# One table of names sets the order of every operation in a fused attention and mixture-of-experts kernel; the change replaces that table

## The chip, the cores and the metric

The kernel runs on one core of one Trainium2 chip. The metric is the time of one execution in microseconds of device time, as the median of several runs; lower is better. Engines are named as the profile names them: PE (matmul), PEld (weight loads for it), DVE (vector), ACT (activation), POOL and SP (the last issues transfers here and computes nothing).

## The reference, cut to what matters

Two parts run one after the other. The first is causal attention over 4 batches, 8 heads, 768 positions and 64 features; four heads in a fixed pattern (`is_retrieval` is 1 for heads 0, 2 and 6) see all earlier positions or, if not flagged, the first 4 and the last 64 only. The second treats the attention's output as 3072 tokens of 512 features and sends them through a soft mixture of 8 experts with 4 slots each.

```
scores = scale * q @ k.T ; a = softmax(where(mask, scores, -1e9)) ; x = a @ v        # per batch and head
logits = x @ phi                                                                      # 3072 x 32
slot_input = softmax(logits, over tokens).T @ x                                       # 32 x 512
slot_out[e] = relu(slot_input[e] @ w1[e]) @ w2[e]                                     # 8 experts
out = softmax(logits, over slots) @ slot_out                                          # 3072 x 512, float32
```

In: q, k and v of 6.3 MB each, w1 and w2 of 16.8 MB each, all float32. Out: 6.3 MB.

## The kernel before, in words

**Stages.** Batches b are 0 to 3. In a batch, heads are worked in pairs (n and n+4), so there are 16 pairs, p = 4b + n. For each pair the scores are made in five groups of two matmuls or more, exponentiated, masked, multiplied with v and normalised. After four pairs of a batch, the logits of the batch are made and its share of the slot inputs is added up. After the last batch come the experts and then the output, in 24 row blocks.

**Transfers in.** Every load of q, k, v and the weights is one instruction on POOL's queue and converts float32 to bfloat16 on the way. There are 12 buffers of 8 KB per partition (`slots`); w2 of experts 4 to 7 goes into memory that attention has left (`qk`, `vx`, `xv`). The last weight, w2 of expert 7, comes in two halves of 256 columns, `Lw15h0` and `Lw15h1`. Stores go out from SP's queue.

**Order.** A class `Plan` collects operations with names, dependences and buffers. Each engine runs its own operations strictly in the order in which their names stand in one string, `ORDER`; a suffix gives the engine where there is a choice (`/A` is ACT, `/D` is DVE, `/P` is POOL):

```
for word in ORDER.split():
    name, _, e = word.partition("/")
    o = by.pop(name)
    o.eng = {"A": "ACT", "D": "DVE", "P": "POOL"}[e] if e else o.engs[0]
```

The order decides also which of several equal buffers an operation gets, since `run` hands them out in that order. Dependences are met by semaphores and do not change.

**Names.** These are used below.

- `Lq0`, `Lk1.32`, `Lw3`: loads (line 244). Lw0 to Lw7 are w1, Lw8 to Lw15 are w2. Raw rows of q, k and v of batches 1 to 3 are packed into shared buffers, so `Lk1.32` and `Lv1.0` fill one buffer together.
- `Tq1.3`, `Eq1.3`: transposes of raw rows on PE (L421) and the copy of their result to `qk` or `xv` (L237 on ACT, L239 on DVE).
- `QK.p.g`, `EX.p.g`, `MK.p.g`: scores of a group (PE, L451), exponential (ACT, L518), mask (DVE, L463). `QX.b`, `EXX.b` are the same for one leftover block per pair (L534).
- `V2.p`, `VB.p`, `VF.p`: v turned to rows (PE, L482), its copy to `vx`, and a masked copy `vf` (L498) for the blocks far from the diagonal. `VF` may run on POOL or DVE.
- `PV.p.i`, `NM.p`: product with v for row block i (PE, L566), normalisation (DVE, L577 and L579).
- `XT`, `XE`, `LG`, `EL`, `TE`, `EG`, `DS`, `SA`: transposes of the attention output, logits, their exponential, and the slot sums (PE L591, L605, L627, L662; ACT L618; DVE L671 and L673).
- `SI`, `H.e.c`, `HR`, `TH`, `HE`: slot inputs, first expert matmul (PE, L734), relu (ACT L744 or DVE L746), transposes (L755) and their copy.
- `W2.e`: second expert matmul (PE, L793); `W2.7.0` and `W2.7.1` need `Lw15h0` and `Lw15h1`. `SO.0`, `SO.1`: its two column halves scaled (ACT, L808, or the same on DVE).
- `EE.b`, `RWa`, `RWRa`: the token weights put in output order, their sums (L778) and reciprocals (L782).
- `OMf0L`, `OEf0L`, `STl0.0`: output matmul of row block 0, left half (PE, L818), its scaling (ACT L824 or DVE L826), and the store (SP, L862). Row blocks 0 to 7 are done in halves L and R; 8 to 23 whole. L needs only `SO.0`. There are 11 stores: four of 256 KB, four of 512 KB, three of 1 MB.
- `Z..`: matmuls on zeros that only keep PE active (L359).

Of the kernel before, what the change touches and what calls it, by code (L numbers as in the profile page):

```python
# [25 lines left out]
QK.1.1 PV.0.3 PV.0.4 QK.1.3 Lk1.32 VF.1/D MK.1.2 EX.1.1 PV.0.5 Lv1.0 QK.2.3 VB.2/D Lv1.64 Tq1.0 NM.0 MK.1.1
EX.1.3 QK.2.4 Tq1.1 PV.1.0 EX.2.3 MK.1.3 PV.1.1 Ek1.0.0/D EX.2.4 QK.1.4 PV.1.2 PV.1.3 QK.2.1 Eq1.0/D Ek1.1.0/D
Eq1.1/D Tq1.2 EX.1.4 QK.2.0 MK.1.4 Tk1.2 Eq1.2/D EX.2.1 Lw1 Ek1.2.0/D PV.1.4 Lw2 VF.2/P Ek1.2.32/D MK.2.3
EX.2.0 Ev1.2.0/A PV.1.5 NM.1 MK.2.0 QK.2.2 Z67 EX.2.2 Tk1.1 Lq2 Ev1.1.0/D Lk2 QK.3.0 Ek1.1.32/D Tk1.0 PV.2.0
VF.3/P QK.3.1 EX.3.0 Ev1.0.0/D Tk1.3 QK.3.2 EX.3.1 Ek1.0.32/D MK.2.2 MK.2.1 Tq1.3 MK.2.4 QK.3.3 Lv2.0 PV.2.1  # L30
PV.2.2 PV.2.3 MK.3.0 EX.3.2 MK.3.1 Lv2.32 QK.3.4 Lq3.0 PV.2.4 PV.2.5 Ev1.3.0/D Ek1.3.0/D EX.3.3 Eq1.3/D EX.3.4
Z65 MK.3.2 NM.2 QK.4.2 QK.4.1 V2.5 PV.3.0 Ek1.3.32/A PV.3.1 MK.3.3 MK.3.4 EX.4.2 V2.4 PV.3.2 QK.4.3 PV.3.3
VB.4/D PV.3.4 PV.3.5 EX.4.1 Lq3.64 QK.4.0 MK.4.2 VB.5/D EX.4.3 XT.2 EX.4.0 NM.3 XT.0 VF.4/P Z66 XE.0/D QK.5.0
MK.4.0 MK.4.1 XE.2/A QK.5.2 EX.5.0 PV.4.0 XT.3 XT.1 PV.4.1 EX.5.2 PV.4.2 XE.3/D QK.4.4 XE.1/D MK.4.3 Tv1.0
Eq2.0/D LG.0 EX.4.4 Tv1.1 Ev1.0.64/D Tv1.3 MK.5.2 EL.0 Ev1.1.64/A MK.5.0 Eq2.1/D QK.5.1 PV.4.3 TE.0 Eq2.3/D
Lw3 QX.1 Ev1.3.64/D EX.5.1 MK.4.4 EXX.1 Tv1.2 EG.0/D DS.0 QK.5.3 VF.5/P MK.5.1 PV.4.4 PV.4.5 Eq2.2/D
Ev1.2.64/A QK.6.2 SA.0 V2.6 EX.5.3 QK.5.4 NM.4 V2.7 VB.6/D PV.5.0 EX.6.2 EX.5.4 Lw4 PV.5.1 QK.6.1 Tk2.0 MK.6.2
EX.6.1 PV.5.2 Lw5 VB.7/D MK.5.3 QK.6.0 Ev2.0.0/D Tk2.1 PV.5.3 QK.6.3 MK.5.4 Ek2.0/D MK.6.1 Lk3 EX.6.0 PV.5.4
EX.6.3 Ek2.1/D Ev2.1.0/D VF.6/P PV.5.5 QK.7.1 Tk2.3 MK.6.0 EX.7.1 QK.6.4 Tk2.2 NM.5 QK.7.0 MK.6.3 Ek2.3/D
Ev2.3.0/D EX.6.4 MK.6.4 PV.6.0 MK.7.1 PV.6.1 Ev2.2.0/D PV.6.2 PV.6.3 QK.7.2 XT.5 PV.6.4 PV.6.5 EX.7.0 XE.5/D  # L40
QK.7.4 MK.7.0 VF.7/P EX.7.2 XT.4 Ek2.2/A NM.6 EX.7.4 XE.4/D QK.7.3 EX.7.3 V2.8 PV.7.0 PV.7.1 MK.7.2 QK.8.0
Tv2.0 PV.7.2 MK.7.4 QK.8.1 VB.8/D Ev2.0.32/D Eq3.0.0/D Tv2.2 EX.8.0 QK.8.2 XT.6 MK.7.3 Ev2.2.32/D EX.8.1
PV.7.3 MK.8.0 XE.6/D Eq3.2.0/D QK.8.3 EX.8.2 EX.8.3 PV.7.4 Lv3 PV.7.5 MK.8.1 NM.7 Tv2.1 QK.9.0 Tv2.3 Eq3.1.0/A
Lw6 VF.8/P QX.2 EX.9.0 Ev2.1.32/D Lw7 Ev2.3.32/D PV.8.0 XT.7 Eq3.3.0/D Lw8 EXX.2 PV.8.1 XE.7/D MK.8.2 QK.8.4
V2.9 VB.9/D V2.11 PV.8.2 EX.8.4 VB.11/A LG.1 MK.8.4 VF.9/P MK.8.3 QK.9.1 PV.8.3 EL.1 V2.10 PV.8.4 VF.11/D
MK.9.0 VB.10/D EX.9.1 QK.9.3 TE.1 PV.8.5 EG.1/D EX.9.3 MK.9.1 QK.9.2 DS.1 QK.9.4 NM.8 Tq3.0 SA.1 EX.9.2 PV.9.0
EX.9.4 PV.9.1 Eq3.0.64/D QK.10.1 XT.8 QK.10.2 Ek3.0/D MK.9.2 XE.8/D Tq3.1 PV.9.2 EX.10.1 MK.9.3 QK.10.0 MK.9.4
Lw9 Ek3.1/D Tq3.2 EX.10.2 PV.9.3 Eq3.2.64/D Ek3.2/D QK.10.3 VF.10/P PV.9.4 PV.9.5 Eq3.1.64/D EX.10.0 MK.10.2
QK.11.0 Tq3.3 EX.10.3 QK.10.4 NM.9 MK.10.0 EX.11.0 Tv3.0 QK.11.2 PV.10.0 MK.10.1 Ev3.0/D PV.10.1 MK.10.3
PV.10.2 EX.10.4 QK.11.1 MK.11.0 MK.10.4 EX.11.2 XT.9 PV.10.3 EX.11.1 Eq3.3.64/D QK.11.4 Lw10 Ek3.3/D PV.10.4  # L50
EX.11.4 XE.9/D PV.10.5 QK.12.1 Tv3.3 EX.12.1 NM.10 QK.11.3 Tv3.2 QK.12.0 EX.11.3 Ev3.3/D PV.11.0 MK.11.1 Tv3.1
EX.12.0 QX.3 Ev3.2/D MK.11.2 XT.10 Ev3.1/D PV.11.1 QK.12.2 EXX.3 MK.11.3 MK.12.0 V2.12 EX.12.2 MK.11.4 VB.12/D
PV.11.2 QK.12.4 MK.12.1 PV.11.3 PV.11.4 EX.12.4 Lw11 XE.10/D QK.12.3 VF.12/P EX.12.3 PV.11.5 QK.13.1 Lw12
NM.11 MK.12.3 V2.13 MK.12.2 QK.13.0 MK.12.4 XT.11 XE.11/D EX.13.1 PV.12.0 PV.12.1 EX.13.0 QK.13.2 PV.12.2
PV.12.3 QK.13.4 EX.13.2 MK.13.0 EX.13.4 PV.12.4 PV.12.5 QK.13.3 LG.2 MK.13.2 NM.12 VB.13/A VF.13/D MK.13.1
EX.13.3 V2.14 QK.14.1 VB.14/D PV.13.0 V2.15 EL.2 EX.14.1 PV.13.1 MK.13.3 QK.14.0 PV.13.2 QK.14.2 VB.15/D
MK.13.4 MK.14.1 Lw13 PV.13.3 EX.14.0 EX.14.2 PV.13.4 VF.14/P VF.15/P QK.14.3 PV.13.5 MK.14.0 QK.14.4 EX.14.3
TE.2 NM.13 EX.14.4 XT.12 EG.2/D QK.15.0 PV.14.0 MK.14.3 PV.14.1 MK.14.2 MK.14.4 XT.13 XE.13/D QK.15.1 PV.14.2
EX.15.0 EX.15.1 PV.14.3 QK.15.2 XE.12/D PV.14.4 PV.14.5 EX.15.2 QK.15.3 EX.15.3 MK.15.1 QK.15.4 MK.15.0 NM.14
MK.15.2 DS.2 PV.15.0 EX.15.4 MK.15.3 PV.15.1 MK.15.4 XT.14 PV.15.2 PV.15.3 Lw14 XE.14/A SA.2 PV.15.4 PV.15.5  # L60
LTa LGa.3 NM.15 XT.15 XE.15/D Z1 LTb ET LGb.3 Z2 EL.3 DS.3 SA.3 RC Z3 SI Z4 SIE EE.3/D H.0.1 H.0.0 EE.0/D
H.1.0 HR.0.1/D HR.0.0/A TH.0 H.1.1 EE.1/D HE.0/D W2.0 W2.1 HR.1.0/A HR.1.1/A Lw15h0 TH.1 HE.1/D W2.2 W2.3 W2.4
EE.2/D W2.5 W2.6 Lw15h1 W2.7.0 SO.0/A RWa RWRa OMf0L OMf1L OEf1L/D RWb OMf2L RWRb OMf3L OMf4L OEf2L/D OEf0L/A
OEf3L/A OMf5L W2.7.1 OEf4L/A OMf6L SO.1/A OMf7L STl0.0 OMf0R OMf1R OMf2R OEf6L/A OEf5L/D OEf1R/A STl0.2 OMf3R
OEf7L/D OEf0R/D OMf4R OMf5R OMf6R STl1.0 OMf7R OMf8 OEf3R/A OMf9 OEf6R/A OEf2R/D OEf4R/D OMf10 OMf11 STl1.2
# [835 lines left out]
```

## Time and profile before

| | |
|---|---|
| median of 3 runs | 149.55 us (149.5 to 149.68) |
| the profiled execution | 149.39 us, of which the span of the trace is 147.6 us |
| PE, DVE, ACT, POOL busy | 128.8, 115.9, 104.9, 36.4 us |
| granted PE clock, mean | 0.964 |
| moved by the transfer queues | 32.89 MB in bytes written, 223 GB/s over the span |

The profiled execution is 1.79 us longer than its span, and 0.16 us shorter than the median. Loads are counted by the bytes that they write (bfloat16), which is half of what they read. Busy time of PE is modelled from pipelined matmuls, so it is no measure of how near PE is to its peak.

### The profile page before, as it was taken

The page shows a single profiled execution, that of the slowest core. Times are in us where ns is not written, and L with a number is a line of the kernel's source. Part 1 is how long each engine was busy: PE and PEld are TensorE (multiplying, and loading weights), DVE is VectorE, ACT ScalarE, POOL GpSimd, SP SyncE. Part 2 cuts the span into 40 slices and gives each one's busy share as a digit, 9 for nine tenths or more (in the row PEclk, how much of TensorE's full clock was granted, in tenths as well). Part 3 has the DMA queues.
Part 4 walks back from the last instruction along what each step waited for, and adds up shares of the span by engine and source line. Part 5 has one row for each costly group of instructions (what it writes and reads, how often), then busy time and mean ns, then how long its engine had stood idle before and what let it go on. Part 6 is the DMA issues. An engine that isn't in the chain of part 4 may idle for free.

```text
span 147.6 us, 5037 instructions
## 1 busy us (share of the span) xinstructions
PE 128.8 (87%) x2196; PEld 82.2 (56%) x2204; DVE 115.9 (78%) x273; ACT 104.9 (71%) x129; POOL 36.4 (25%) x59
## 2 busy tenths in 40 slices
...
DMA  3999999999999999999999999999999999889995
GB/s 31 197 217 220 216 208 213 212 222 215 212 212 214 214 216 223 220 215 209 206 218 220 213 215 215 218 218 218 215 215 218 218 206 190 119 276 361 422 413 233
DMA packets 10373, 32.89 MB, mean 223 GB/s; under 512 B 1392, under 2 KB 5488, under 8 KB 8048
## 3 DMA queue, kind: packets, MB, share of 16 engines
...
q14 instruction: 4, 0.03, 0.1%
...
## 4 chain that ended last, share of the span: by engine, by line
PE 34%; DMA 24%; DVE 18%; ACT 8%; POOL 4%; issue 4%; ACTq 0%; POOLq 0%; DVEq 0%
DMA slot<-in_v_dram 12%; DMA qk<-in_moe_w_dram 12%; PE ps L566 9%; PE ps L451 8%; PE ps L421 7%; DVE pt L463 6%; ACT pt L518 4%; DVE xv L579 4%; ACT slot L824 3%; PE ps L818 2%; POOL slot L244 2%; PE ps L591 2%; PE ps L605 2%; DVE vx L239 1%; DVE qk L239 1%
## 5 line engine op out<-in xcount | busy, mean ns | idle before, releaser
L518 ACT ACTIVATE pt<-ps 128x1024 bf16<-128x1024 f32 x80 | 77.4, 1035 | 8.0 <-PE ps L451 7.2
L463 DVE TENSOR_TENSOR pt<-pt,msk 128x512 bf16<-128x512 bf16 (+1 forms) x80 | 38.2, 505 | 0.7 <-ACT pt L518 0.7
L451 PE MATMUL ps<-qk 64*128 64x512 bf16 (+3 forms) x256 | 32.5, 309 | 0.2
L566 PEld LDWEIGHTS <-pt 128*128 128x128 bf16 x640 | 25.1, 97 | 9.4 <-issue 6.2
L566 PE MATMUL ps<-vx,pt 128*128 128x65 bf16 x352 | 28.5, 193 | 1.0 <-DVE pt L463 0.4
L421 PE MATMUL ps<-ident,slot 128*64 128x128 bf16 (+1 forms) x640 | 22.8, 216 | 2.6 <-DMA slot<-in_q_dram 1.1
L498 POOL TENSOR_TENSOR vf<-vx,fm 128x528 bf16<-128x528 bf16 x12 | 13.9, 1164 | 44.5 <-DVE vx L239 42.1
L421 PEld LDWEIGHTS <-slot 128*64 128x64 bf16 (+1 forms) x640 | 17.7, 109 | 10.7 <-issue 8.7
L566 PE MATMUL ps<-vf,pt 128*128 128x65 bf16 x288 | 22.8, 195 | 0.0
L239 DVE COPY qk<-ps 128x768 bf16<-128x768 bf16 (+2 forms) x35 | 15.3, 466 | 6.0 <-PE ps L421 4.8
L359 PE MATMUL ps<-zero 128*128 128x512 bf16 x51 | 15.2, 412 | 1.8 <-DVE zero L350 1.2
L579 DVE TENSOR_TENSOR xv<-ps,rs 128x768 bf16<-128x768 f32 x16 | 15.3, 957 | 0.6
L451 PEld LDWEIGHTS <-qk 64*128 64x128 bf16 x256 | 9.3, 94 | 8.2 <-issue 2.7
L239 DVE COPY xT<-ps 128x768 bf16<-128x768 bf16 (+1 forms) x16 | 8.9, 569 | 3.2 <-PE ps L755 2.3
L244 POOL DMA_DIRECT2D slot<-in_moe_w_dram x12 | 7.1, 589 | 14.5 <-PE ps L421 12.0
L824 ACT ACTIVATE slot<-ps,rrow 128x512 f32<-128x512 f32 (+1 forms) x17 | 8.8, 588 | 2.2 <-PE ps L818 2.2
L826 DVE TENSOR_SCALAR slot<-ps,rrow 128x256 f32<-128x256 f32 (+1 forms) x15 | 8.5, 603 | 1.8 <-PE ps L818 1.1
L818 PE MATMUL ps<-msk,xv 128*128 128x256 bf16 (+1 forms) x31 | 8.0, 381 | 1.7 <-ACT slot L824 0.9
L239 DVE COPY xv<-ps 128x768 bf16<-128x768 bf16 (+2 forms) x21 | 8.9, 430 | 0.7 <-PE ps L421 0.4
L359 PEld LDWEIGHTS <-zero 128*128 128x128 bf16 x58 | 5.3, 103 | 7.5 <-issue 2.7
L237 ACT COPY qk<-ps 128x768 bf16<-128x768 bf16 (+1 forms) x5 | 3.5, 713 | 7.0 <-PE ps L421 7.0
L239 DVE COPY vx<-ps 128x768 bf16<-128x768 bf16 x14 | 7.7, 553 | 0.6 <-PE ps L482 0.6
...
## 6 DMA issues: line engine op xcount, KB each, us to landing
slot<-in_moe_w_dram POOLq DMA_DIRECT2D x12, 1024.0 KB, 22.7
out_dram<-slot SPq DMA_DIRECT2D x3, 1024.0 KB, 6.2
...
qk<-in_moe_w_dram POOLq DMA_DIRECT2D x1, 1024.0 KB, 19.1
```

The costliest lines, as they stand in the source:

```text
L239: nc.vector.tensor_copy(dst, src)
L244: emit=lambda o: e.dma_start(dst(), src))
L359: nc.tensor.matmul(scb[buf.slot][:, 0, :], zero[:, 0:128], zero, start=True, stop=True)
L421: nc.tensor.transpose(t[64 * i:64 * (i + 1), :, s, :], rv[:, i, 8 * c + s, :], ident[0:rows, 0:rows])
L451: nc.tensor.matmul(scb[sc.slot][:, i, c:c + 128 * nb], kk, qq.rearrange("p b c -> p (b c)"), start=True, stop=True)
L463: e.tensor_tensor(pT[:, :, 0:w], pT[:, :, 0:w], mh[:, :, c:c + w], op=ALU.mult)
L498: e.tensor_tensor(vfs[VFb[p].slot], vv, mm, op=ALU.mult)
L518: nc.scalar.activation(pTs[PTb[b, n].slot][:, :, 512 * g:512 * (g + 1)], scb[sc.slot], ACT.Exp, scale=scale)
L566: nc.tensor.matmul(pvb[:, h, 65 * i:65 * (i + 1)], lt, rhs, start=(j == 0), stop=(j == i))
L579: nc.vector.tensor_tensor(xo, pvw[:, :, :, 0:64], r.rearrange("p i (j o) -> p i j o", o=1).to_broadcast([P, 2, 6, 64]), op=ALU.mult)
L818: nc.tensor.matmul(bank()[:, b0:b0 + c1 - c0], out_lhs(gi, r), slot_out[:, c0:c1], start=True, stop=True)
L824: nc.scalar.activation(d, s_, ACT.Copy, scale=sc_)
```

## The change

The string `ORDER` is replaced. The set of names is the same, and so is the order of names on SP's queue and of the loads among themselves. All other code is untouched. The first of the 48 rows:

```
-zero Lri warm Lq0 tables ident keypos Tq0.3 Tq0.2 Eq0.3/A Eq0.2/A Z0 Tq0.0 flags hm0 Lk0 hm3 Tq0.1 Lv0
+Lri Lphi0 zero Lq0 tables ident warm Lk0 Tq0.3 keypos flags Tq0.2 hm3 Lphi1 Z64 Eq0.3/D Eq0.2/D Tq0.1 Tq0.0
```

Fifty operations change their engine. Of the four `VF` that were on DVE (pairs 0, 1, 11 and 13) all go to POOL, which now has 16. The four `EE` go from DVE to ACT. `SO.1` and `OEf22`, `OEf23` go from ACT to DVE. The copies `Eq`, `Ek` and `Ev` are mixed anew: 10 of 64 on ACT, which were 8.

**On ACT at the start**, the copies of q and k of batch 0 (`qk_75`) and the first exponentials. Before:

```order
L237 ACT_TABLE_LOAD
L237 COPY qk_75<-ps 128x24x32 x2
L383 CAST phi_89<-eT 128x512
L518 ACTIVATE pt<-ps 128x2x512 x7
L534 ACTIVATE vx_78<-ps 128x1024
```

After:

```order
L237 ACT_TABLE_LOAD
L237 COPY qk_75<-ps 128x24x32 x3
L383 CAST phi_89<-eT 128x512
L237 COPY qk_75<-ps 128x24x32
L518 ACTIVATE pt<-ps 128x2x512 x8
L534 ACTIVATE vx_78<-ps 128x1024
```

Two of the four copies of k move to ACT beside two on DVE, and two of the copies of q change places with DVE's.

**On POOL towards the end of the loads**: `slot10_73` to `xv_80` are the buffers of Lw9 to Lw14, `qk1_76` that of the two halves of Lw15, `vf` the masked copies. Before:

```order
L244 DMA slot10_73<-in_moe_w2_dram 128x4096
L498 TENSOR_TENSOR vf2_83<-vx0_78,fm_87 128x528
L244 DMA slot11_74<-in_moe_w2_dram 128x4096
L244 DMA slot5_68<-in_moe_w2_dram 128x4096
L498 TENSOR_TENSOR vf0_81<-vx1_79,fm_87 128x528
L244 DMA qk0_75<-in_moe_w2_dram 128x4096
L244 DMA vx0_78<-in_moe_w2_dram 128x4096
L498 TENSOR_TENSOR vf1_82<-vx1_79,fm_87 128x528
L498 TENSOR_TENSOR vf0_81<-vx1_79,fm_87 128x528
L244 DMA xv_80<-in_moe_w2_dram 128x4096
L244 DMA qk1_76<-in_moe_w2_dram 128x8x256 x2
```

After:

```order
L498 TENSOR_TENSOR vf0_81<-vx0_78,fm_87 128x528
L244 DMA slot10_73<-in_moe_w2_dram 128x4096
L244 DMA slot11_74<-in_moe_w2_dram 128x4096
L244 DMA slot4_67<-in_moe_w2_dram 128x4096
L244 DMA qk0_75<-in_moe_w2_dram 128x4096
L498 TENSOR_TENSOR vf1_82<-vx1_79,fm_87 128x528
L498 TENSOR_TENSOR vf2_83<-vx1_79,fm_87 128x528
L244 DMA vx0_78<-in_moe_w2_dram 128x4096
L498 TENSOR_TENSOR vf0_81<-vx1_79,fm_87 128x528
L498 TENSOR_TENSOR vf1_82<-vx1_79,fm_87 128x528
L244 DMA xv_80<-in_moe_w2_dram 128x4096
L244 DMA qk1_76<-in_moe_w2_dram 128x8x256 x2
```

Lw13 (`vx0_78`) now stands behind two masked copies, those of pairs 12 and 13, instead of one; Lw9 stands behind that of pair 11.

**On ACT at the end**, from the exponentials of the last batch's logits (L618) over the relus (L744) to the output. Before:

```order
L618 ACTIVATE eT,csum<-ps 128x768
L744 ACTIVATE msk<-ps,emask 128x512 x3
L808 ACTIVATE msk<-ps,rcs 128x256
L824 ACTIVATE slot_66<-ps,rrow 128x256 x2
L824 ACTIVATE slot_70<-ps,rrow 128x256
L808 ACTIVATE msk<-ps,rcs 128x256
L824 ACTIVATE slot_70<-ps,rrow 128x256
L824 ACTIVATE slot_66<-ps,rrow 128x256 x2
```

After:

```order
L618 ACTIVATE eT,csum<-ps 128x768
L237 COPY xv<-eT 128x4x192 x2
L744 ACTIVATE msk<-ps,emask 128x512 x2
L237 COPY xv<-eT 128x4x192 x2
L808 ACTIVATE msk<-ps,rcs 128x256
L824 ACTIVATE slot_66<-ps,rrow 128x256 x2
L824 ACTIVATE slot_70<-ps,rrow 128x256 x4
L824 ACTIVATE slot_66<-ps,rrow 128x256 x2
```

The four `EE` copies (L237 from `eT`) now stand on ACT around the relus, one relu and `SO.1` (the second L808) have left it, and six left-half scalings follow `SO.0` in one piece.

On PE, `TH.1` moves from behind `W2.1` to behind `W2.0`, and the first transposes that need `Lk1.32` and `Lv1.0` (`Tk1.2`) now stand behind `Tq1.3`, `PV.1.4`, `PV.1.5`, `QK.2.2` and `QK.3.3`, which all came after them before.

More of the change, by code (lines that the diff above doesn't have):

```diff
@@ L26 @@
[L26 to L65, printed above, removed]
```

54 lines of the change are left out of this document (47 added, 7 removed).

## Prediction

> **What bounds the kernel now.** I read the page's slices first, then the chain that ended last, then stretches of the span, and then the rows around the last loads.
>
> ```profile
> span 147.6 us, 5037 instructions
> DMA  3999999999999999999999999999999999889995
> xv<-in_moe_w_dram POOLq DMA_DIRECT2D x1, 1024.0 KB, 13.3
> 12.88 18.41 DMA slot<-in_v_dram
> 112.01 17.10 DMA qk<-in_moe_w_dram
> ```
>
> The transfer engines are 90% busy or more in nearly every slice from the second on. The third row is Lw14: 1 MB, landing 13.3 us after its issue. The chain (start, length, what) has two long transfers in it: Lv1.0 until 31.3 us and Lw15h1 from 112.0 until 129.1 us. Between them the chain runs through attention, where the columns below are stretch, length, then busy time and count of PE, PEld, DVE, ACT and POOL, the granted PE clock, the transfer share and GB/s.
>
> ```profile
> 5.00:120.00 115.00, 109.71 (x1963) 71.83 (x1972) 101.67 (x244) 92.06 (x107) 33.16 (x49) 1.00 1.05 215
> 15.00:32.00 17.00, 15.14 (x271) 9.46 (x270) 15.31 (x38) 14.41 (x15) 5.86 (x8) 1.00 1.05 214
> 32.00:113.00 81.00, 79.19 (x1453) 54.07 (x1454) 75.48 (x171) 74.10 (x85) 21.89 (x28) 1.00 1.04 215
> 90.00:110.00 20.00, 19.39 (x330) 12.98 (x326) 18.96 (x42) 19.97 (x24) 5.23 (x6) 1.00 1.03 216
> 126.50:131.00 4.50, 3.66 (x53) 2.24 (x53) 2.71 (x8) 2.97 (x7) 0.00 (x0) 0.92 0.66 141
> 131.00:135.50 4.50, 3.98 (x14) 1.75 (x14) 3.72 (x7) 3.16 (x8) 0.00 (x0) 0.70 1.01 343
> 135.50:146.00 10.50, 1.61 (x6) 0.48 (x5) 2.39 (x4) 3.55 (x7) 0.00 (x0) 0.74 1.02 415
> ```
>
> Loads run at 215 GB/s for 115 us with no gap, and stores at 343 and then 415 GB/s with no gap after 131 us. Attention is nearly full on three engines as well (PE 79.2 of 81 us), so two bounds lie close together. Where they meet decides, and that is the wait of the second expert matmul for the last weight:
>
> ```profile
> 122.05 1.05 PE L793 MATMUL ps<-slot,xT 128*32 128x256 bf16 x32
> 123.03 0.71 PE L755 MATMUL ps<-ident,msk 128*128 128x128 bf16 x8
> 122.27 0.69 ACT L744 ACTIVATE msk<-ps,emask 128x512 bf16<-128x512 f32 x1 [0.92 <-PE ps L734]
> 125.42 0.61 PE L793 MATMUL ps<-xv,xT 128*32 128x256 bf16 x16
> 126.54 0.40 PE L793 MATMUL ps<-qk,xT 128*32 128x256 bf16 x8 [0.51 <-DMA qk<-in_moe_w_dram]
> 126.99 0.47 ACT L808 ACTIVATE msk<-ps,rcs 128x256 bf16<-128x256 f32 x1 [4.03 <-PE ps L793]
> 129.15 0.40 PE L793 MATMUL ps<-qk,xT 128*32 128x256 bf16 x8 [0.24 <-DMA qk<-in_moe_w_dram]
> ```
>
> W2.6 (the row of `xv`) ends at 126.03. W2.7.0 starts at 126.54, after 0.51 us of waiting for Lw15h0; W2.7.1 starts at 129.15, when Lw15h1 has landed. So everything before is 0.51 us early, and from there on the output waits for transfers.
>
> **The loads (cost 0).** They keep their order and their bytes, the first one keeps its place at the head of POOL's queue, and so their end moves only if the queue runs dry. POOL issues them, and the rows that leave least room are these:
>
> ```profile
> 85.42 0.58 POOL L244 DMA_DIRECT2D slot<-in_moe_w_dram  x1 [6.39 <-PE ps L421]
> 91.64 0.53 POOL L244 DMA_DIRECT2D slot<-in_moe_w_dram  x1 [5.64 <-PE ps L421]
> 95.54 0.54 POOL L244 DMA_DIRECT2D vx<-in_moe_w_dram  x1
> 101.95 2.52 POOL L498 TENSOR_TENSOR vf<-vx,fm 128x528 bf16<-128x528 bf16 x2 [5.86 <-DVE vx L239]
> 110.54 0.59 POOL L244 DMA_DIRECT2D xv<-in_moe_w_dram  x1 [6.08 <-PE ps L662]
> ```
>
> Lw14 goes out at 110.54 and lands 13.3 us later, at 123.84. Its own 1.05 MB take 4.9 us at 215 GB/s, so it still stood 8.4 us behind others. Counting bytes issued against bytes moved, I make the backlog 1.06 MB then, 4.9 us, and at least 2 MB (9 us) at Lw10 and Lw11. After the change Lw13 stands behind `VF.12` and `VF.13`. `VF.13` ran on DVE at 100.21 (the last row of the next fence), so on POOL I put it between 98 and 101, and Lw13 3 to 6 us later than 95.54; its predecessors have bytes until about 110. Lw9 waits for `VF.11`, 5 us later than before, against a queue that lasts until 91. Lw14 still waits for DS.2, which keeps its place ahead of PV.15.0. Between 0 (taken, since the smallest reserve is 4.9 us) and, if DS.2 came 6 us late, 1.1 us more.
>
> **Attention (cost 0, a gain in cover).** Three things become shorter. The copies of k for batch 0 are shared by two engines:
>
> ```profile
> 12.89 1.02 DVE L239 COPY qk<-ps 128x768 bf16<-128x768 bf16 x2 [0.46 <-PE ps L421]
> 14.45 1.02 DVE L239 COPY qk<-ps 128x768 bf16<-128x768 bf16 x2 [0.53 <-PE ps L421]
> 16.08 0.39 PE L451 MATMUL ps<-qk 64*128 64x512 bf16 x2
> 8.70 1.50 ACT L237 COPY qk<-ps 128x768 bf16<-128x768 bf16 x2 [6.69 <-PE ps L421]
> 31.43 0.64 PE ps L421 x16
> 32.06 0.79 PE ps L566 x22
> 32.85 0.32 PE ps L451 x2
> 100.21 0.71 DVE L498 TENSOR_TENSOR vf<-vx,fm 128x528 bf16<-128x528 bf16 x1
> ```
>
> DVE makes a copy in 0.51 us and ACT in 0.75, two at a time instead of one; I put the first scores 0.75 us earlier (16.08 to about 15.3). Second, Tq1.3 (0.64), PV.1.4 and PV.1.5 (0.79 together), QK.2.2 and QK.3.3 (0.32 each) now stand ahead of Tk1.2, which waited for Lv1.0 until 31.43: 2.07 us of PE work. PE is idle for 17 - 15.14 = 1.86 us in that stretch and starts 0.75 us sooner, so there is room for it. Third, four `VF` at 0.71 us leave DVE, 2.8 us; on POOL one takes some 1.2 us (the two above took 2.52), which is idle 75% of the time. ACT's load in attention stays: two more small copies, one fewer large XE and VB each. If PE keeps its 98% after 32 us, attention ends 1 to 2 us earlier. All of it lies in cover: W2.7.0 still starts when Lw15h0 lands, so I count 0. What is late next is that load.
>
> **The experts (cost 0).** `TH.1` ahead of `W2.1`: it starts when HR.1.1 (the ACT row, to 122.96) is done, at 123.0 as before, so W2.1 is pushed behind it and PE waits 0.5 us. That puts W2.6 some 0.3 to 0.45 us later, and 0.51 us covers it; 0.1 to 0.2 us of reserve are left if attention ends when it did. `EE` on ACT (four copies of 768 elements, 0.75 us each as its copies of that size in the fence above) fits before 126.5, since ACT waits 4.03 us there for PE ahead of `SO.0` (the row at 126.99). `HR.1.0` on DVE stands behind `HE.0` and ends near 122.7, still ahead of HR.1.1.
>
> **The output (taken +0.1).** The rows are a store's issue on SP's queue and the scalings:
>
> ```profile
> 128.50 0.41 SPq L862 DMA_DIRECT2D out_dram<-slot  x1
> 129.05 1.02 SPq L862 DMA_DIRECT2D out_dram<-slot  x1
> 132.68 0.58 SPq L862 DMA_DIRECT2D out_dram<-slot  x1
> 139.07 0.44 SPq L862 DMA_DIRECT2D out_dram<-slot  x1
> L824 ACT ACTIVATE slot<-ps,rrow 128x256 f32<-128x256 f32 x8 | 3.5, 471 | 1.1 <-PE ps L818 1.1
> L826 DVE TENSOR_SCALAR slot<-ps,rrow 128x256 f32<-128x256 f32 x8 | 3.8, 477 | 1.2 <-PE ps L818 1.1
> ```
>
> With 0.47 us a half block, ACT does 0L, 2L, 4L, 5L, 7L, 6L from 127.83 and DVE 1L and 3L: the first store goes out at 128.50 as before, the second near 128.95, the fourth near 130.7. The right halves 1R, 2R, then 4R, 7R, 6R follow on ACT, so the sixth store would leave near 133.1 instead of 132.68, while the last (20 to 23) is ready some 0.5 us sooner, since ACT and DVE share the whole blocks more evenly. The transfer engines are full at 343 GB/s, and a 512 KB store takes them 1.5 us, so a store that is up to 0.4 us late is mostly hidden. Between -0.1 and +0.3; I take +0.1.
>
> **The sum.** 149.39 (the profiled execution) + 0 + 0 + 0 + 0.1 = 149.5. The median of the runs stands 0.16 higher, and with that the forecast is 149.6 us. A change within 0.2% (0.3 us) is about what a measurement of this kernel cannot tell from none, so this is "same", 149.25 to 149.85.
>
> **Rivals.**
>
> Attention ends late (slower, 16%). Place: the stretch 90 to 110 us, where ACT has 0.03 us left in 20, and PE 0.6. Each engine runs strictly in its new order, so one wait of PE for a mask or of ACT for a score is lost for good. It decides once the end of attention comes over 0.5 us late, since 0.2 us of reserve are left; 1.2 us late would give 149.6 + 1.0 = 150.6. For it: no engine has slack. Against it: the 2.07 us pulled ahead of the load at 31 us.
>
> A colder PE (slower, 10%). The profile shows it already:
>
> ```profile
> 128.00:130.00 2.00, 1.62 (x25) 0.85 (x23) 1.49 (x5) 1.53 (x5) 0.00 (x0) 1.00 0.56 133
> 130.00:132.00 2.00, 1.87 (x8) 1.21 (x9) 1.82 (x4) 1.52 (x5) 0.00 (x0) 0.56 0.83 276
> ```
>
> The clock falls to about half just after 130 us, though PE counts as busy for most of the 4.5 us before. If attention ends 1 to 2 us earlier, PE idles that long ahead of 126.54, and the fall may come some us sooner: W2.7.0 and W2.7.1 (0.40 each) and the left blocks would take up to twice as long, 0.3 to 0.5 us on the way to the first stores: 150.0. Against it: the zero matmuls before and the same work. [...]
>
> The queue runs dry (slower, 4%): DS.2 or a `VF` over 4.9 us late; 151 or more.
>
> The output closes its gap (faster, 22%). In 126.5 to 131 us the transfers have a share of 0.66 only. Stores at full rate from 129.15 on, 2.1 MB of half rows at 343 and 4.2 MB at 415 GB/s, take 16.2 us and would end at 145.4 instead of about 146: at most 0.6 us, 149.0. For it: the second store comes 0.1 us sooner and ACT is free of `SO.1`. Against it: SP's row of 1.02 us stays, and the gap begins with the landing of the last load.
>
> **How the numbers follow.** Same 0.48; faster 0.22; slower 0.16 + 0.10 + 0.04 = 0.30. From the closed gap (149.0, with 0.1 for its own spread) to 1.1 us beyond the forecast (attention 1.3 us late) lie 8 in 10: 148.9 to 150.7.
>
> **What would show it.** Right: the wait of W2.7.0 for `qk<-in_moe_w_dram` grows to 1.5 us or more, its start stays within 0.3 us of 126.54, Lw14 still lands well ahead of Lw15, and the share from 131 us on stays at 1.0. Wrong: W2.7.0 waits for nothing and starts late (attention), a clock below 1.0 before 130 us, a stretch of loads under 200 GB/s before 120 us (dry queue), or a start of W2.7.0 well before 126.3, by which loads would not be pinned to their bytes.

## The result, and the profile after

| | before | after |
|---|---|---|
| median | 149.53 us (6 runs, 149.26 to 150.03) | 151.32 us (6 runs, 151.15 to 153.14) |
| the profiled execution, its span | 149.39, 147.6 | 151.38, 149.6 |
| granted PE clock, mean | 0.964 | 0.978 |

The ratio is 1.0135, with a 95% interval of 1.0086 to 1.0184. By the medians the kernel is slower by 1.8 us. The forecast of 149.6 (148.9 to 150.7) was wrong, and its rival "attention ends late" is what happened, at nearly twice the price that I gave it.

These are the slices and stretches of the kernel after, with the columns as in the prediction:

```profile
span 149.6 us, 5037 instructions
DMA  2999999999999999999999999999999999379995
5.00:120.00 115.00, 109.06 (x1932) 71.50 (x1930) 99.48 (x234) 94.34 (x108) 36.99 (x52) 1.00 1.05 215
15.00:32.00 17.00, 15.42 (x273) 9.58 (x272) 15.09 (x36) 14.13 (x16) 8.19 (x13) 1.00 1.05 213
32.00:113.00 81.00, 76.79 (x1389) 51.85 (x1386) 74.18 (x166) 72.43 (x83) 22.87 (x30) 1.00 1.04 216
126.50:131.00 4.50, 4.17 (x129) 3.71 (x120) 1.33 (x4) 3.38 (x6) 0.00 (x0) 1.00 0.40 56
131.00:135.50 4.50, 3.85 (x27) 1.88 (x27) 3.55 (x9) 4.32 (x12) 0.00 (x0) 1.00 0.84 277
```

The loads run as before, 215 GB/s until 120 us. In the stretch from 32 to 113 us PE is busy for 76.79 us instead of 79.19: 2.40 us are lost there. After 126.5 us the transfer engines, not PE, wait: their share is 0.40, because the first store goes out at 130.90 instead of 128.50. The clock stays at 1.00 until 135.5.

PE's rows with their waits show where the 2.40 us went, and what came of it (the seventh row is DS.3, at 115.75 before; the last is W2.7.0, at 126.54 before):

```profile
25.93 0.20 PE L566 MATMUL ps<-vx,pt 128*128 128x65 bf16 x1 [1.26 <-DVE pt L463]
48.62 0.60 PE L566 MATMUL ps<-vx,pt 128*128 128x65 bf16 x6 [0.77 <-DVE pt L463]
82.16 0.34 PE L566 MATMUL ps<-vx,pt 128*128 128x65 bf16 x6 [1.10 <-DVE xv L579]
98.28 0.34 PE L566 MATMUL ps<-vx,pt 128*128 128x65 bf16 x6 [0.57 <-DVE xv L579]
108.66 0.34 PE L566 MATMUL ps<-vx,pt 128*128 128x65 bf16 x6 [0.58 <-DVE xv L579]
113.05 0.22 PE L566 MATMUL ps<-vx,pt 128*128 128x65 bf16 x2 [0.45 <-DVE xv L579]
118.26 0.61 PE L662 MATMUL ps<-xv,elg 128*32 128x512 bf16 x6
128.80 0.51 PE L793 MATMUL ps<-qk,xT 128*32 128x256 bf16 x8
```

PE waits for DVE, for a mask or for a normalisation that stands behind masks, in places where the kernel before had no wait over 0.3 us. From 16 to 114 us its waits for DVE add up to 5.1 us, and to 1.5 us in the kernel before; it never waits for POOL in either. The attention ends 2.51 us later, the cover of 0.51 us is used up, and W2.7.0 starts 2.26 us late without waiting for its load.

**The work pulled ahead at the start.** The prediction let the first scores start at 15.3 us and saw 2.07 us of PE's work done while `Tk1.2` waited for its load. These rows of PE are the matmuls on zeros ahead of the first scores, the first scores (at 16.08 before), and `Tk1.2` (at 31.43 before):

```profile
14.84 1.47 PE L359 MATMUL ps<-zero 128*128 128x512 bf16 x6
16.24 0.39 PE L451 MATMUL ps<-qk 64*128 64x512 bf16 x2
33.44 0.64 PE L421 MATMUL ps<-ident,slot 128*64 128x128 bf16 x16
```

The first scores come 0.16 us later, not 0.75 sooner: in both kernels they stand behind the last transposes of k and six matmuls on zeros. `Tk1.2` starts 2.01 us later, with 2.07 us more work done ahead of it, so there is no lead to speak of.

**What DVE was doing.** The next rows are from DVE and POOL of the kernel after, around the two longest of these waits, and around a normalisation beside a `VF`:

```profile
46.84 2.06 DVE L463 TENSOR_TENSOR pt<-pt,msk 128x512 bf16<-128x512 bf16 x2
47.19 1.08 POOL L498 TENSOR_TENSOR vf<-vx,fm 128x528 bf16<-128x528 bf16 x1
78.00 1.76 DVE L463 TENSOR_TENSOR pt<-pt,msk 128x512 bf16<-128x512 bf16 x2
78.24 3.66 POOL L498 TENSOR_TENSOR vf<-vx,fm 128x528 bf16<-128x528 bf16 x3 [7.72 <-DVE vx L239]
80.15 0.82 DVE L463 TENSOR_TENSOR pt<-pt,msk 128x512 bf16<-128x512 bf16 x1
80.89 0.22 DVE L577 RECIPROCAL rs<-ps 128x12 f32<-128x12 f32 x1
97.18 1.06 POOL L498 TENSOR_TENSOR vf<-vx,fm 128x528 bf16<-128x528 bf16 x1 [1.17 <-DVE vx L239]
97.27 0.96 DVE L579 TENSOR_TENSOR xv<-ps,rs 128x768 bf16<-128x768 f32 x1
```

Each of the two pairs of masks, which took 2.06 and 1.76 us, ran beside a `VF` on POOL. A mask of 128x512 alone takes 0.41 us, and one of 128x768, as the second at 78.00 is, 0.55; the first mask at 46.84 took 1.73 by itself, the longest of all 80. The trace's single records say it more exactly. Of the 80 masks, 17 overlap a `VF` in time: 11 of them took 0.75 to 1.73 us, and six, all begun 0.09 to 0.24 us before the `VF`, kept their 0.41 to 0.55. None of the other 63 took more than 0.43 (128x512) or 0.56 us (128x768). The normalisation at 97.27, with one input from PSUM (`ps`), takes its usual 0.96 us beside a `VF`, and so do two others; twelve copies from PSUM (L239) beside a `VF` keep their time too: 0.28 us with 256 elements, 0.41 to 0.42 with 512, 0.54 to 0.56 with 768, as away from one. So a mask, whose two inputs both lie in SBUF, seems to stand still while a `VF` runs. I call this the lock below. That it is the place of the inputs which decides is my reading of these records; in the profiles before and after, no instruction whose only input lies in SBUF ran on DVE beside a `VF`.

The profile before had it too, and I did not read it there (DVE, beside the POOL row at 101.95 in the prediction; then the group of all masks of that shape before and after):

```profile
102.71 2.37 DVE L463 TENSOR_TENSOR pt<-pt,msk 128x512 bf16<-128x512 bf16 x3
L463 DVE TENSOR_TENSOR pt<-pt,msk 128x512 bf16<-128x512 bf16 x64 | 28.4, 466 | 0.7 <-ACT pt L518 0.7
L463 DVE TENSOR_TENSOR pt<-pt,msk 128x512 bf16<-128x512 bf16 x64 | 30.1, 497 | 1.0 <-ACT pt L518 1.0
```

Three masks of 0.41 took 2.37 us. With 416 ns as the undisturbed mean (e6, below), the 64 masks lost 64 x 50 ns = 3.2 us before and 64 x 81 ns = 5.2 us after; the 16 masks of 128x768 lost another 1.8 us in each. What differs more is the place: before, little of the lost time lay ahead of something that PE waited for, and PE's longest wait for DVE was 0.28 us (at 75.86, behind a mask beside `VF.9`).

### The profile page after: what moved, and what is told of

It reads as the page before. It is cut to its first block, busy times and chain, and to the rows that moved or that the text cites. A ratio compares the mean times of both kernels' runs of the same rounds, so it can differ in the third digit from the quotient of the medians.

```text
span 149.6 us, 5037 instructions
## 1 busy us (share of the span) xinstructions
PE 129.1 (86%) x2204; PEld 82.5 (55%) x2204; DVE 113.6 (76%) x265; ACT 110.6 (74%) x133; POOL 40.8 (27%) x63
## 5 line engine op out<-in xcount | busy, mean ns | idle before, releaser
L463 DVE TENSOR_TENSOR pt<-pt,msk 128x512 bf16<-128x512 bf16 (+1 forms) x80 | 39.9, 530 | 1.1 <-ACT pt L518 1.0
L566 PE MATMUL ps<-vx,pt 128*128 128x65 bf16 x352 | 28.0, 193 | 4.8 <-DVE xv L579 2.7
L498 POOL TENSOR_TENSOR vf<-vx,fm 128x528 bf16<-128x528 bf16 x16 | 18.2, 1147 | 39.5 <-DVE vx L239 32.7
L239 DVE COPY qk<-ps 128x768 bf16<-128x768 bf16 (+2 forms) x34 | 14.7, 458 | 5.0 <-PE ps L421 4.5
L359 PE MATMUL ps<-zero 128*128 128x512 bf16 x58 | 17.4, 435 | 1.2 <-DVE zero L350 1.2
L579 DVE TENSOR_TENSOR xv<-ps,rs 128x768 bf16<-128x768 f32 x16 | 15.3, 957 | 0.6
L239 DVE COPY xT<-ps 128x768 bf16<-128x768 bf16 (+1 forms) x17 | 9.6, 567 | 4.3 <-PE ps L755 2.7
L239 DVE COPY xv<-ps 128x768 bf16<-128x768 bf16 (+2 forms) x20 | 8.5, 430 | 2.1 <-PE ps L421 1.8
L824 ACT ACTIVATE slot<-ps,rrow 128x256 f32<-128x256 f32 (+1 forms) x19 | 9.3, 567 | 0.8 <-PE ps L818 0.7
L239 DVE COPY vx<-ps 128x768 bf16<-128x768 bf16 x15 | 8.2, 549 | 1.2 <-PE ps L482 1.1
L826 DVE TENSOR_SCALAR slot<-ps,rrow 128x512 f32<-128x512 f32 (+1 forms) x13 | 7.8, 643 | 1.7 <-PE ps L818 1.5
L818 PE MATMUL ps<-msk,xv 128*128 128x256 bf16 (+1 forms) x32 | 6.5, 325 | 2.2 <-DVE slot L826 1.5
```

Of the source, the lines that this page charges most:

```text
L239: nc.vector.tensor_copy(dst, src)
L359: nc.tensor.matmul(scb[buf.slot][:, 0, :], zero[:, 0:128], zero, start=True, stop=True)
L463: e.tensor_tensor(pT[:, :, 0:w], pT[:, :, 0:w], mh[:, :, c:c + w], op=ALU.mult)
L498: e.tensor_tensor(vfs[VFb[p].slot], vv, mm, op=ALU.mult)
L566: nc.tensor.matmul(pvb[:, h, 65 * i:65 * (i + 1)], lt, rhs, start=(j == 0), stop=(j == i))
L579: nc.vector.tensor_tensor(xo, pvw[:, :, :, 0:64], r.rearrange("p i (j o) -> p i j o", o=1).to_broadcast([P, 2, 6, 64]), op=ALU.mult)
```

## The experiments

In the diffs, `+` and `-` lines are words of `ORDER` unless they are code. Ratios are to the kernel before, measured beside each.

**Which part carries the loss: e3 and e4.** The two orders were cut at the end of the last attention stage and joined crosswise.

```
e3:  - LGa.3 NM.15 LTa ... STf5.0 (the order after)    + LTa LGa.3 NM.15 ... STf5.0 (the order before)
e4:  - LTa LGa.3 NM.15 ... STf5.0 (the order before)   + LGa.3 NM.15 LTa ... STf5.0 (the order after)
```

> The changed order up to the logits of the last batch (LTa, LGa.3), then the order before for everything from there on (last transposes, experts, output). If attention carries the loss (lock or order theory): 150.9 to 151.4 us, with the second expert matmul starting 1.9 to 2.3 us later than the 126.5 of before. If experts and output carry it: 149.4 to 149.8.

> The order before up to the logits of the last batch, then the changed order for experts and output. If attention carries the loss: 149.3 to 149.8 us, W2.7.0 still waiting for its load near 126.5, by 0.1 to 0.3 us instead of 0.5. If experts and output carry it: 150.8 to 151.4.

Measured: e3 151.41 us, 1.0122 [1.0092, 1.0152]; e4 150.10 us, 1.0029 [1.0014, 1.0044]. The attention carries the loss. The tail alone costs 0.4 us (0.2 to 0.7), which neither forecast of e4 had; since e3 is as slow as the kernel after, the two costs don't add up.

**Is it the four `VF` that moved: e1, e2 and e9.**

```
e1 (after):   - VF.0 VF.1 VF.11 VF.13 on POOL   + VF.0/D VF.1/D VF.11/D VF.13/D
e2 (before):  - VF.0/D VF.1/D VF.11/D VF.13/D   + VF.0/P VF.1/P VF.11/P VF.13/P
e9 (before):  - VF.11/D VF.13/D                 + VF.11/P VF.13/P
```

> The changed order, with VF.0, VF.1, VF.11 and VF.13 back on DVE at the places where their names stand. Lock theory (a masked copy on POOL holds up a mask on DVE for as long as it runs, and the four added ones stand where PE needs the mask at once): the wait of 1.26 us before PV.0.4 near 25.9 us goes, and part of the 1.10 us at 82.2; DVE takes 2.8 us of work back in a stretch where it is not always busy: 149.9 to 150.5 us, and masks (128x512) at 465 to 480 ns in the mean instead of 497. Order theory (the new order itself makes PE, ACT and DVE wait, wherever VF runs): 151.2 us or more, since DVE has 2.8 us more to do.

> The order before, with VF.0, VF.1, VF.11 and VF.13 on POOL instead of DVE, at their places. Lock theory: masks slow from 466 to some 495 ns in the mean, DVE gains 2.8 us and loses about 2; slower by 0.3 to 2 us, 149.8 to 151.5. Order theory: no slower than 149.8, since DVE is relieved and nothing else moves.

> The order before, with only VF.11 and VF.13 on POOL instead of DVE, so that no load stands behind a masked copy that comes late (in the run with four, VF.0 and VF.1 stood ahead of Lq1 and Lv1.0 and the loads fell to 151 GB/s between 15 and 32 us). Lock theory: the two cost up to 1.2 us of masks standing still each and save 0.7 each, with 0.5 us of cover by the load: between 149.4 and 150.3. Order theory: 149.4 to 149.7.

Measured: e1 150.90 us, 1.0088 [1.0058, 1.0119]; only 0.4 us came back, less than the lock theory forecast and more than the order theory. The waits of PE at 48, 82 and 98 us stayed at 0.71, 1.11 and 0.57 us, since they lie beside `VF.5`, `VF.10` with `VF.9`, and `VF.12`, which were on POOL before as well; that at 108 us fell to 0.17. The wait of 1.26 us at 25.9 went as forecast, but PE waited 0.82 us for a load of k at 26.38 in its place. e2 took 154.91 us, 1.0347 [1.0312, 1.0383], but for another reason. In the order before, `VF.0` and `VF.1` stand ahead of Lq1 and Lv1.0 on POOL's queue, and the loads starved (the stretch from 15 to 32 us):

```profile
15.00:32.00 17.00, 11.99 (x193) 7.42 (x193) 11.52 (x29) 10.54 (x11) 9.76 (x14) 0.89 0.79 151
```

151 GB/s instead of 214: this is the rival of the dry queue, in a kernel where it can be seen, and it says nothing on the lock. e9 has only the two later ones: 149.72 us, 1.0007 [0.9989, 1.0025]. The attention ended 0.72 us later (DS.3 at 116.47), and W2.7.0 started at 126.77 without waiting for its load: the delay was just covered by the reserve. `VF.11` now runs on POOL directly behind `VF.9`, and the three masks beside them (0.41, 0.41 and 0.55 us alone) take 2.98 us, so that PE waits 1.15 us for them, instead of 0.28:

```profile
73.78 2.27 POOL L498 TENSOR_TENSOR vf<-vx,fm 128x528 bf16<-128x528 bf16 x2 [4.76 <-DVE vx L239]
73.82 2.98 DVE L463 TENSOR_TENSOR pt<-pt,msk 128x512 bf16<-128x512 bf16 x3 [0.19 <-ACT pt L518]
76.52 0.20 PE L566 MATMUL ps<-vx,pt 128*128 128x65 bf16 x1 [1.15 <-DVE pt L463]
```

On average one `VF` more or less on POOL moves the end of the attention by 0.15 us (e1) to 0.36 us (e9); which one it is, and beside what, matters more.

**Can the waits be cured by order: e8.** The normalisations that PE waited for were moved ahead of masks and copies.

```
e8 (after):  NM.8 to right behind PV.8.5; NM.11 to right behind PV.11.5; PV.14.5 to right ahead of QK.15.3
```

> The changed order, with three moves and all masked copies as they are: NM.8 on DVE ahead of VB.11 and MK.9.1, NM.11 ahead of MK.12.1, MK.12.2 and VB.13, and PV.14.5 on PE ahead of QK.15.3. Both theories say that PE waited 1.10, 0.57 and 0.45 us for these normalisations: if these waits are the loss, it falls by 1.2 to 2.0 us, to 149.4 to 150.2. If the waits only move to the work that was passed (masks and copies now later), it stays at 150.8 to 151.4. Lock theory adds that masks keep their mean of 490 to 500 ns.

Measured: 151.74 us, 1.0139 [1.0117, 1.0161], above every forecast. The mean mask fell to 476 ns, but PE's waits at 82 and 98 us stayed (0.92 and 1.26 us): it now waited for the copies that had been moved back.

**Other `VF` on DVE: e12.** These four lie beside the masks that stood ahead of PE's waits.

```
e12 (after):  - VF.5 VF.9 VF.10 VF.15 on POOL   + VF.5/D VF.9/D VF.10/D VF.15/D
```

> The order after, with VF.5, VF.9, VF.10 and VF.15 on DVE: the four beside which a mask stood still just ahead of a wait of PE (48.6, 82.2 and 108.7 us). The first four, which the change had moved, gave back 0.4 us. If it matters where the lock falls: the waits at 48.6 and 82.2 shrink below 0.5 us each, W2.7.0 starts at or before 127.9 and the time is 150.2 to 150.6. If only the number of masked copies on POOL counts: 150.9 as with the first four. If DVE, which gets four pieces of about 0.7 us, is the bound: 151.3 to 151.8.

Measured: 153.08 us, 1.0222 [1.0203, 1.0241], above every forecast as well. The lock's theory was right on the wait at 48 us, which vanished; that at 108 us stayed at 0.63. At 82 us two `VF` now stood on DVE ahead of NM.8 (DVE, then PE):

```profile
79.36 1.57 DVE L498 TENSOR_TENSOR vf<-vx,fm 128x528 bf16<-128x528 bf16 x1
80.86 0.22 DVE L577 RECIPROCAL rs<-ps 128x12 f32<-128x12 f32 x1
82.12 0.34 PE L566 MATMUL ps<-vx,pt 128*128 128x65 bf16 x6 [1.93 <-DVE xv L579]
```

Beside `VF.11` on POOL (79.29 to 80.37) a `VF` on DVE, 0.70 alone, takes 1.57 us: its two inputs lie in SBUF too. The profiled execution took 151.58 us, the lowest of seven, so the rest up to 153.08 is not explained by it. That stays open.

**The lock with the work left out: e6 and e7.** `VF` writes 2 of its 66 columns of the first block only. The rest of `vf` keeps the ones that a second edit, not shown, writes there once at the start, so the output is not the attention's.

```
-e.tensor_tensor(vfs[VFb[p].slot], vv, mm, op=ALU.mult)
+e.tensor_tensor(vfs[VFb[p].slot][:, :, 0:1, 0:2], vv[:, :, 0:1, 0:2], mm[:, :, 0:1, 0:2], op=ALU.mult)
```

> The changed order, with each masked copy on POOL cut to its first block and two of 66 columns (the rest of vf is filled once at the start), so that POOL holds nothing up for long; the output is not the attention's. Lock theory (masks on DVE stand still while a masked copy runs on POOL, and with the changed order that hits masks and normalisations that PE waits for: 0.77 us at 48.6, 1.10 at 82.2, 0.57 at 98.3, 0.58 at 108.7, 1.26 at 25.9): those waits go, masks 128x512 come to 415 to 425 ns, attention ends 2.5 to 3.5 us earlier, W2.7.0 waits for its load again, and the time falls to 149.2 to 150.1 us. Order theory (the waits come from the places of the operations on PE, ACT and DVE alone): 151.0 us or more.

> The order before, with the same cut of the masked copies. Both theories: attention was already early enough for the last load, so the time stays within 0.4 us of 149.55; masks come to 415 to 425 ns from 466, and W2.7.0 waits longer than 0.51 us for its load. Under the lock theory this kernel and the changed order with the same cut differ by no more than the 0.5 us that the changed experts and output cost.

Measured: e6 149.99 us, 1.0028 [1.0004, 1.0051]; e7 151.16 us, 1.0080 [1.0044, 1.0117]. In both the masks run undisturbed (416 ns in the mean); the group of e6, and W2.7.0 of e6 and of e7:

```profile
L463 DVE TENSOR_TENSOR pt<-pt,msk 128x512 bf16<-128x512 bf16 x64 | 25.1, 416 | 1.3 <-ACT pt L518 1.1
127.06 0.40 PE L793 MATMUL ps<-qk,xT 128*32 128x256 bf16 x8 [1.78 <-DMA qk<-in_moe_w_dram]
126.82 0.40 PE L793 MATMUL ps<-qk,xT 128*32 128x256 bf16 x8 [2.02 <-DMA qk<-in_moe_w_dram]
```

With `VF` cut short the last normalisation stands at 111.27 us in the order after (114.96 with the whole `VF`) and at 111.10 in the order before (112.51). So the whole `VF` costs the attention 3.7 us in the one order and 1.4 in the other (where four of them are on DVE), and without it the two orders are equal within 0.17 us: the new one had no lead to give. That e7 became slower was expected by neither theory, and its runs fall into two groups, two near 150.0 and four at 151.1 to 151.5; the profile is of the second. PE stands still for 2.02 us, and its clock is halved from 130 on; W2.7.1 also came 1.8 us late, at 130.98, since its load landed then. Why that load was late isn't shown. Both made the stores late:

```profile
129.00:130.00 1.00, 0.18 (x1) 0.09 (x1) 0.69 (x2) 0.67 (x2) 0.00 (x0) 0.75 0.29 94
132.00:135.00 3.00, 2.97 (x12) 1.53 (x11) 2.65 (x6) 2.23 (x6) 0.00 (x0) 0.50 0.38 127
```

**The lock with all work kept: e16, e17 and e18.** Each `VF` is written as four instructions. e18 has besides the order before from the last attention stage on.

```
-e.tensor_tensor(vfs[VFb[p].slot], vv, mm, op=ALU.mult)
+for j in range(4): e.tensor_tensor(vfs[VFb[p].slot][:, :, j:j + 1, :], vv[:, :, j:j + 1, :], mm[:, :, j:j + 1, :], op=ALU.mult)
```

> The order after, each VF written as four instructions on POOL of 132 columns instead of one of 528, the same work. If a mask stands still for as long as the POOL instruction that it meets lasts: the longest mask falls from 1.7 to about 0.8 us, and masks may slip in between the pieces, so the waits of PE at 48.6, 82.2, 98.3 and 108.7 us shrink; W2.7.0 starts at 127.3 to 128.3 and the time is 150.2 to 150.9. If a mask that is held stays held until POOL has nothing more to issue: longest mask about as before or above (1.7 us or more), 151.2 to 151.6. If POOL's shorter instructions cost much more in sum (over 1.6 us for the four), a later VF: 151.5 to 152.5.

> The order after with each VF in four pieces, and from the last attention stage on the order before: both causes of the loss taken away at once. The attention stage of the pieced kernel ended at 115.96 us (DS.3), and the tail before took 10.3 us from there to the end of W2.6, so W2.7.0 is ready at 126.2 and waits for its load as in the kernel before (126.5 to 126.9). If lock and experts are all of the loss: 149.3 to 149.6, no longer apart from the kernel before. If there is a third cause: 149.8 to 150.3.

> The order before, with the twelve VF on POOL and the four on DVE written as four instructions each. In the order before no mask that stands still is ahead of something PE waits for, and 0.5 us are in reserve ahead of W2.7.0. If shorter pieces only free DVE: mean mask below 0.45 us, time 149.4 to 149.7, the same. If four short instructions on DVE cost more than one (0.7 us): slower, 149.7 to 150.3.

Measured: e16 149.66 us, 1.0008 [0.9994, 1.0022]; e18 149.58 us, 0.9998 [0.9985, 1.0010]. The groups of the masks and of `VF` in e16, its DS.3 and W2.7.0:

```profile
L463 DVE TENSOR_TENSOR pt<-pt,msk 128x512 bf16<-128x512 bf16 x64 | 27.6, 457 | 1.2 <-ACT pt L518 1.1
L498 POOL TENSOR_TENSOR vf<-vx,fm 128x132 bf16<-128x132 bf16 x64 | 28.3, 471 | 33.4 <-DVE vx L239 27.6 <-ACT vx L237 5.5 <-PE ps L566 0.2
115.96 0.61 PE L662 MATMUL ps<-xv,elg 128*32 128x512 bf16 x6
126.88 0.40 PE L793 MATMUL ps<-qk,xT 128*32 128x256 bf16 x8 [0.19 <-DMA qk<-in_moe_w_dram]
```

Nothing but the length and number of POOL's instructions has changed, and POOL even works longer (28.3 us instead of 18.2 in the 16 whole ones). Still the attention ends 2.3 us earlier, W2.7.0 waits for its load again, and 1.66 us of the 1.8 are back, more than I had forecast. The longest mask of 128x512 fell from 1.73 us to 0.63. Of the wider ones (0.55 alone) the longest fell only from 1.43 to 1.35: it met all four pieces of `VF.7`, so a mask may be caught more than once. The start of normalisations (L577) shows step by step where the time had gone:

| start, us | NM.5 | NM.7 | NM.8 | NM.10 | NM.11 | NM.12 | NM.13 | NM.15 |
|---|---|---|---|---|---|---|---|---|
| before | 60.17 | 70.27 | 77.94 | 88.85 | 95.00 | 98.98 | 105.00 | 112.51 |
| after | 59.55 | 71.90 | 80.89 | 90.53 | 97.02 | 101.73 | 107.39 | 114.96 |
| after, in pieces (e16) | 59.22 | 71.57 | 79.60 | 89.25 | 95.28 | 100.00 | 105.08 | 112.65 |
| after less e16 | 0.33 | 0.33 | 1.29 | 1.28 | 1.74 | 1.73 | 2.31 | 2.31 |

The last row rises only at NM.8, NM.11 and NM.13 (and once before NM.5): just where PE waited at 48, 82, 98 and 108 us. So at these four places 2.31 of the 2.45 us came back. The pieces help the order before as well, by 0.59 us (112.51 to 111.92 in e17), so that with pieces in both the order after still ends 0.73 us later.

**The tail: e13, e14 and e15.**

```
e13 (e4):      - EE.1/A EE.2/A EE.3/A EE.0/A      + EE.1/D EE.2/D EE.3/D EE.0/D, in the same places
e14 (before):  from W2.7.0 on the order after
e15 (before):  LTa to W2.6 in the order after, from W2.7.0 on the order before
```

> The order before up to the last attention stage and the order after from there on (150.10 before this edit), with the four EE copies on DVE instead of ACT. If the EE on ACT (1.6 us each against 0.88 on DVE) cost the 0.5 us: 149.5 to 149.75. If it is the order of the output's row blocks: 150.0 to 150.2.

> The order before up to W2.6, and from W2.7.0 on the order after (the output's row blocks, their scalings and SO.1 on DVE, with RWRa and RWRb later). If the +0.5 us of the changed tail lies in the output: 150.0 to 150.2, with the rate between 129 and 130 us at 60 to 100 GB/s instead of 184. If it lies in the experts: 149.5 to 149.7.

> The counterpart: the order before up to the last attention stage, the experts in the order after (EE on ACT, TH.1 behind W2.0), and from W2.7.0 on the order before. If the +0.5 us lies in the output: 149.5 to 149.7. If it lies in the experts: 150.0 to 150.2.

Measured: e13 150.18 us, 1.0038 [1.0023, 1.0053]; e14 149.90 us, 1.0017 [1.0002, 1.0032]; e15 149.94 us, 1.0026 [1.0015, 1.0036]. e13 decided nothing, since on DVE the copies stood ahead of `SIE` and PE waited 1.44 us for that. e15 shows what the experts cost (W2.6, W2.7.0, and the `EE` on ACT):

```profile
126.42 0.61 PE L793 MATMUL ps<-xv,xT 128*32 128x256 bf16 x16
126.89 0.55 PE L793 MATMUL ps<-qk,xT 128*32 128x256 bf16 x8
123.43 3.20 ACT L237 COPY xv<-eT 128x768 bf16<-128x768 bf16 x2
```

From DS.3 (116.33 in this execution, 0.58 later than before) to the end of W2.6 it is 10.70 us, 0.42 more than before (115.75 to 126.03), and W2.7.0 has no wait left. Each half of the tail costs 0.25 to 0.4 us when it is set into the kernel before. In the profile of e14 PE waits 0.82 us for the load and its clock is 0.5 from 129.4 us, so part of its 0.25 may be that and not the output's order. Set behind the pieced attention, both halves together cost 0.08 us by the medians (e16 against e18), which can't be told from nothing. The tail's share therefore stays open between 0 and 0.4 us.

**The colder PE: e10, e11 and e19.** Matmuls on zeros are added where PE waits for the last weight: 8 in e7, 2 in the kernel before, 4 in e17.

```
 ORDER:  W2.5 W2.6 + Z7 Lw15h1 W2.7.0
+fill('Z7', 8, [w2o[-3]])       # e10 on e7;  2 in e11 on before;  4 in e19 on e17
```

> The order before with the short VF (first block only, 2 of 66 columns, so vf is left mostly unfilled), and eight more matmuls on zeros on PE between W2.6 and W2.7.0 (8 x 0.22 = 1.8 us), where PE stood still for 2.02 us waiting for its load. If the colder PE made the short VF slower in the order before (clock 0.50 from 130 to 136 us, 151.16): clock 1.00 in that stretch, L818 matmuls back to 0.22 us each, 149.4 to 149.9. If the later landing of the second half of w2 did it (W2.7.1 at 130.98 instead of 129.15): W2.7.1 stays near 131 and the time stays at 150.8 to 151.3.

> The order before, with two matmuls on zeros (0.44 us) on PE between W2.6 and W2.7.0, where PE waited 0.51 us for the load. If the clock in 130 to 133.5 us (0.50 in the profile before) costs time: granted clock at or above 0.97 and 149.3 to 149.45, 0.1 to 0.3 us below the kernel before. If the stores bind that stretch alone: 149.5 to 149.7, the same.

> The order before with each VF in four pieces (150.14 without the fill, PE standing still for 1.11 us ahead of W2.7.0, clock 0.50 from 129 to 132 us), and four more matmuls on zeros (0.88 us) between W2.6 and W2.7.0. If the wait made PE cold and the cold PE made the time: clock 1.00 to 131 us or longer and 149.4 to 149.7. If the pieces themselves cost it: 150.0 to 150.3.

Measured: e17 150.14 us, 1.0038 [1.0024, 1.0051], and with the fill (e19) 149.80 us, 1.0014 [1.0003, 1.0025]. e17 is the order before with pieces. Its four `VF` on DVE take longer in pieces (0.92 us, one 1.54, instead of 0.70), but its attention still ends 0.6 us sooner (last normalisation at 111.92); PE waits 1.11 us for the load, and the kernel is slower. Two microseconds of each, e17 first:

```profile
129.00:130.00 1.00, 0.71 (x9) 0.27 (x9) 0.45 (x1) 0.45 (x3) 0.00 (x0) 0.52 0.53 179
130.00:131.00 1.00, 0.97 (x5) 0.55 (x4) 0.52 (x2) 0.79 (x2) 0.00 (x0) 0.50 0.50 164
129.00:130.00 1.00, 0.80 (x11) 0.42 (x11) 0.72 (x2) 0.79 (x3) 0.00 (x0) 1.00 0.22 73
130.00:131.00 1.00, 0.76 (x6) 0.39 (x4) 0.76 (x2) 0.90 (x3) 0.00 (x0) 1.00 1.03 332
```

With the fill the clock stays at 1.00, and the stores reach 332 GB/s a microsecond earlier, behind a slower one (73 GB/s instead of 179); from 133 to 134 us they run at 328 instead of 258. That brings 0.34 of the 0.6 us, between the two forecasts; the rest isn't explained. e10 (149.71 us, 1.0030 [0.9999, 1.0061]) points the same way against e7's 151.16, but its runs spread from 149.30 to 152.51, so it settles nothing on the late load of e7. e11 took 149.55 us, 0.9995 [0.9985, 1.0006]: the kernel before with a clock of 1.00 from 130 to 134 us, instead of 0.50 to 0.67, is no faster. There the stores fill the transfer engines in any case (a share of 0.99 to 1.04 from 131 to 134 us in both); in these two pairs the colder PE cost time only where it came ahead of them.

The clock went with the wait in the other profiles too. Where PE waited 0.51 us or more for Lw15h0 and nothing filled the wait (before 0.51, e18 0.69, e14 0.82, e17 1.11, e7 2.02), the clock fell to 0.5 at 2.5 to 3.7 us behind the start of W2.7.0. Where it waited 0.25 us or less (after, e9 and e15 not at all, e16 0.19, e4 0.25), it was 1.00 until 143.1 us in the kernel after, until 135.5 at least in e4, e15 and e16, and until 131 at least in e9.

## Why the prediction was wrong

- **Loads, 0: right.** Their rate and order stayed, and Lw15h0 and Lw15h1 landed at 126.50 and 129.13 us, as before (126.50 and 129.11). By the packets of POOL's queue the backlog at Lw14 was 1.41 MB before, not the 1.06 of the prediction, so the reserve was larger than I put it.
- **Attention, 0: wrong, and this is the step that failed.** I moved four `VF` to POOL "which is idle 75% of the time" and counted their time as gone from DVE. A `VF` on POOL wasn't free for DVE: of the 17 masks beside one, 11 took 0.75 to 1.73 us instead of 0.41 to 0.55. No term of the sum had a price for that. "If PE keeps its 98%" was the condition, and PE kept 76.79 of 81 us, 94.8%. The four moved `VF` themselves are only 0.4 us of it (e1); the rest came because the new order put `VF.5`, `VF.9`, `VF.10`, `VF.12` and `VF.15` beside masks ahead of a wait of PE. The lead at 31 us, put at 2.07 us, was 0.06: `Tk1.2` ran at 33.44 instead of 31.43. The idle time of PE that was to hold this work was still there (1.58 us from 15 to 32 us instead of 1.86), now mostly as the wait of 1.26 us at 25.93, behind masks beside `VF.0` and `VF.1`. The lock isn't all of that: in e1, e6 and e16 this wait is gone, PE waits 0.36 to 1.35 us for a load of k there, and `Tk1.2` still starts at 33.3 to 33.8. The first scores weren't earlier because DVE's copies of k were not what they waited for; the prediction's own rows show DVE idle for PE (0.46 and 0.53 us) ahead of them. With `VF` cut short both orders end within 0.17 us, so even the gain in cover wasn't in the order.
- **Experts, 0: size right, cover wrong.** 0.3 to 0.45 us were forecast and 0.42 measured. The `EE` were taken at 0.75 us on ACT, a figure of copies from PSUM, and took 1.6 (3.20 for two). They did fit. The reserve of 0.51 us that was to cover the experts had gone to the attention.
- **Output, +0.1 (to +0.3): within the range as far as e14 tells it**, 0.2% of 149.5, or 0.25 us, with an interval of 0.03 to 0.5. What part of it is the colder PE isn't shown.
- **The rivals.** "Attention ends late" had its mechanism (a wait of PE for a mask is lost for good) and its threshold of 0.5 us right, but not what makes the masks late. Its chance of 16% and its 1.2 us were too low; the attention was 2.5 us late and the kernel lost 1.8. "A colder PE" was priced about right at 150.0 (e17 150.14, e19 149.80), but it needs an early attention, which the change didn't have. In e17 1.11 us of waiting were followed by a clock of 0.52 from 129 to 130 us. The dry queue was seen only in e2. The gap of the output didn't close: the share from 126.5 to 131 us is 0.40 instead of 0.66, and the rate from 131 to 135.5 us is 277 GB/s instead of 343.

No kernel here beats the one before by more than can be told; e18, with 0.9998, equals it.
